# Attention over 512 heads on one core: chunks of 8 heads loaded in runs of three, and matmuls that use weights already in the array

## Chip, cores and metric

The kernel runs on one core of a Trainium2 chip. The metric is the device time of one execution in microseconds (us). The core has a matmul engine (PE, with its weight loads listed apart as PEld), a vector engine (DVE), a scalar engine (ACT), GpSimd (POOL), and SyncE (SP), which here only issues DMAs. The DMAs run on 16 engines that all queues share.

## The reference

For each of 16 x 32 = 512 heads, 192 queries attend to 1024 keys, with 128 elements a head, in bf16:

```python
B, H, Sq, Sk, D = 16, 32, 192, 1024, 128
scale = q.shape[-1] ** -0.5
scores = jnp.einsum("bhqd,bhkd->bhqk", q, k) * scale
p = _softmax(scores, axis=-1)
return jnp.einsum("bhqk,bhkd->bhqd", p, v)
```

## The kernel before

**Units.** Two heads a and b have 2 x 192 = 384 query rows. They are worked on as three units of 128 rows: unit `k3 = 0` has the first 128 rows of a, unit 1 the last 128 rows of b, and unit 2 the 64 rows left over from each, side by side in the two halves of the array (`tile_position` (0,0) and (0,64)). Three units make a pair of heads; there are 256 pairs and `NU` = 768 units.

**What happens to a unit.** PE multiplies queries by keys into `s_ps` (`qk`, lines 246, 253, 259: two matmuls of 512 columns, or four of half the array). DVE scales them into `ss` and takes the row extreme `nb` (line 335). Then half of the units (`route` R_W, never `k3 = 2`) go through POOL, which subtracts (line 210), and the others through ACT, which takes the exponential and the row sum (line 391), both into `x_sb`. PE transposes `x_sb` in eight blocks into `pt_ps` (`tr`, line 275). ACT moves that to `pt_sb` (line 402 with the exponential for R_W units, line 404 as a copy). PE multiplies with v into `o_ps` (`pv`, eight products, line 302, or twice eight in the array's halves, lines 308 and 310). For R_W units each of the eight is followed by a product of the same weights with one column of ones, which sums the rows (line 305). DVE divides each finished pair by its sums into `ob` (`onorm`, lines 362 and 365).

**Order on PE.** It is written out by hand: step `t` issues `qk(t+1)`, `tr(t-4)`, `pv(t-7)` (`LAGS`). `s_ps`, `pt_ps` and `o_ps` have two buffers each, `ss` four, `x_sb` four and `pt_sb` four. Each engine waits on counting semaphores (`s_qk`, `s_max`, `s_xp`, `s_xa`, `s_tr`, `s_eva`, `s_pv`, `s_on`) for its inputs and for free buffers. Every `pe.matmul` and `pe.transpose` becomes a weight load and a matmul; a wait that stands in front is on the load.

**Loads and stores.** Heads are taken in groups of `G` = 16 (32 groups of 24 units) and `kt`, `qt`, `vs` and `ob` have two slots each (`NS`, `NSO`). SP issues everything, in program order: k and q by a transposing DMA (`load_kq`, lines 144 and 148), v by a plain copy (`load_v`, line 155), the results from `ob` (`stores`, line 173). The k and q load of group g+2 waits until `qk` of group g is finished, its v load until `pv` of group g is finished. Group 0 is loaded in three parts (`FIRST`: heads 0 to 2, 2 to 8, 8 to 16). In the steady state SP's order is k, q and v of group g+2, then the store of group g:

```python
for g in range(NGR):
    if g + NS < NGR:
        loads(g + NS)
    for a, b in (LAST if g == NGR - 1 else ((0, PPG),)):
        stores(g, a, b)
```

Of the kernel before, what the change touches and what calls it, by code (L numbers as in the profile page):

```python
# [10 lines left out]
R_EA = 0  # L11
# [1 line left out]
R_W = 2  # L13


def _attention_kernel(nc, q, k, v, out, G=16, NS=2, LAGS=(2, 4, 5, 7), ROUTES=(R_W, R_W, R_EA, R_W, R_EA, R_EA),
                      FIRST=((0, 2), (2, 8), (8, 16)), LAST=((0, 4), (4, 6), (6, 7), (7, 8))):
    B, H, SQ, D = q.shape
    SK = k.shape[2]
    assert D == 128 and SK == 1024 and SQ == 192, (D, SK, SQ)  # L20
# [11 lines left out]
    NSS = L_X + 2  # L32
    NX = L_TR - L_X + 2
    NPT = L_PV - L_EV + 2
    NSO = 2
    NRS = 4

    qf = q.rearrange("b h s d -> (b h) s d")
# [25 lines left out]
    with ExitStack() as es:  # L64
# [74 lines left out]
        @block.sync  # L139
        def _(e):  # L140
            def load_kq(g, a, b, sems):
                s = g % NS
                h0 = g * G
                e.dma_start_transpose(  # L144
                    kt[:, s, :, a * 128:b * 128],
                    kf[h0 + a:h0 + b].rearrange("g (p t) d -> (g p) (t d)", t=KT_TILES),
                ).then_inc(sems[0], 16)
                e.dma_start_transpose(  # L148
                    qt[:, s, a * SQ:b * SQ],
                    qf[h0 + a:h0 + b].rearrange("g r d -> (g r) d"),  # L150
                ).then_inc(sems[1], 16)

            def load_v(g, a, b, sm):
                h0 = g * G
                e.dma_start(  # L155
                    vs[:, g % NS, a:b],
                    vf[h0 + a:h0 + b].rearrange("g (p t) d -> p g t d", t=KT_TILES),
                ).then_inc(sm, 16)

            def loads(g):  # L160
                s = g % NS
                last_u = (g - NS + 1) * UPG - 1
                if g >= NS:
                    e.wait_ge(s_qk, last_u + 1)
                load_kq(g, 0, G, (sxk[s], sxq[s]))
                if g >= NS:
                    e.wait_ge(s_pv, last_u + 1)
                load_v(g, 0, G, svl[s])

            def stores(g, a, b):  # L170
                so = g % NSO
                e.wait_ge(s_on, g * PPG + b)
                e.dma_start(
                    of[g * G + 2 * a:g * G + 2 * b].rearrange("h r d -> (h r) d").rearrange(
                        "(n p) d -> p n d", p=128),
                    ob[:, so, a:b].rearrange("p pg y d -> p (pg y) d"),
                ).then_inc(sst[so], 16)

            n = len(FIRST)
            for i in range(n):  # L180
                load_kq(0, *FIRST[i], (sf[i], sf[i]))
                if i > 0:
                    for i2 in range(i if i > 1 else 0, i + 1):
                        load_v(0, *FIRST[i2], sfv[i2])
            for g in range(1, min(NS, NGR)):
                loads(g)
            for g in range(NGR):
                if g + NS < NGR:
                    loads(g + NS)
                for a, b in (LAST if g == NGR - 1 else ((0, PPG),)):  # L190
                    stores(g, a, b)
            for so in range(min(NSO, NGR)):
                n_uses = len(range(so, NGR, NSO))
                if so == (NGR - 1) % NSO:
                    n_uses += len(LAST) - 1
                e.wait_ge(sst[so], 16 * n_uses)
# [21 lines left out]

        @block.tensor
        def _(pe):  # L220
            def qk(u):
                pr, k3, g, pg = unit_info(u)
                s = g % NS
                a = 2 * pg
                b = 2 * pg + 1
                if g == 0:
                    for i, (h, _) in enumerate(FIRST):
                        if u == 3 * h // 2:
                            pe.wait_ge(sf[i], 32)
                elif u % UPG == 0:  # L230
                    pe.wait_ge(sxk[s], load_cnt(g))
                    pe.wait_ge(sxq[s], load_cnt(g))
                if u >= 2:
                    pe.wait_ge(s_max, u - 1)
                S = s_ps[u % 2]
                ins = None
                for c in range(2):
                    cs = slice(4 * c, 4 * c + 4)

                    def keys(x):  # L240
                        return kt[:, s, cs, x * 128:x * 128 + 128]

                    if k3 < 2:
                        x = a if k3 == 0 else b
                        x0 = a * SQ if k3 == 0 else b * SQ + 64
                        ins = pe.matmul(  # L246
                            S[:, cs],
                            qt[:, s, x0:x0 + 128],
                            keys(x),
                            start=True, stop=True,  # L250
                        )
                    else:
                        pe.matmul(  # L253
                            S[0:64, cs],
                            qt[:, s, a * SQ + 128:a * SQ + 192],
                            keys(a),
                            start=True, stop=True, tile_position=(0, 0),
                        )
                        ins = pe.matmul(  # L259
                            S[64:128, cs],  # L260
                            qt[:, s, b * SQ:b * SQ + 64],
                            keys(b),
                            start=True, stop=True, tile_position=(0, 64),
                        )
                ins.then_inc(s_qk, 1)

            def tr(u):
                wait_x(pe, u)
                if u >= 2:
                    wait_evac(pe, u - 2)  # L270
                X = x_sb[:, u % NX, :]
                PT = pt_ps[u % 2]
                ins = None
                for t in range(KT_TILES):
                    ins = pe.transpose(PT[:, t, :], X[:, t * 128:t * 128 + 128], ident[:])  # L275
                ins.then_inc(s_tr, 1)

            def pv(u):
                pr, k3, g, pg = unit_info(u)
                s = g % NS  # L280
                if g == 0:
                    for i, (h, _) in enumerate(FIRST):
                        if u == 3 * h // 2:
                            pe.wait_ge(sfv[i], 16)
                elif u % UPG == 0:
                    pe.wait_ge(svl[s], load_cnt(g))
                wait_evac(pe, u)
                if k3 == 0 and pr >= 2:
                    pe.wait_ge(s_on, pr - 1)
                O = o_ps[pr % 2]  # L290
                PTS = pt_sb[:, u % NPT]
                sl = O_SLOT[k3]
# [1 line left out]
                b = 2 * pg + 1  # L294
                ins = None
                with_rs = route(u) == R_W
                for t in range(KT_TILES):
                    first = t == 0
                    last = t == KT_TILES - 1
                    if k3 < 2:  # L300
                        x = a if k3 == 0 else b
                        ins = pe.matmul(O[:, sl, :], PTS[:, t, :], vs[:, s, x, t, :],  # L302
                                        start=first, stop=last, skip_group_check=True)
                        if with_rs:
                            ins = pe.matmul(O[:, 3, sl: sl + 1], PTS[:, t, :], ones[:, 0:1],  # L305
                                            start=False, stop=last, skip_group_check=True)
                    else:
                        pe.matmul(O[0:64, sl, :], PTS[:, t, 0:64], vs[:, s, a, t, :],  # L308
                                  start=first, stop=last, skip_group_check=True, tile_position=(0, 0))
                        ins = pe.matmul(O[64:128, sl, :], PTS[:, t, 64:128], vs[:, s, b, t, :],  # L310
                                        start=first, stop=last, skip_group_check=True, tile_position=(0, 64))
                        if with_rs:
                            pe.matmul(O[0:64, 3, sl: sl + 1], PTS[:, t, 0:64], ones[:, 0:1],
                                      start=False, stop=last, skip_group_check=True, tile_position=(0, 0))
                            ins = pe.matmul(O[64:128, 3, sl: sl + 1], PTS[:, t, 64:128], ones[:, 0:1],
                                            start=False, stop=last, skip_group_check=True, tile_position=(0, 64))
                ins.then_inc(s_pv, 1)

            pe.wait_ge(s_setup, 2)
# [1 line left out]
            for step in range(NU + L_PV):  # L321
                if step + 1 < NU:
                    qk(step + 1)
                if 0 <= step - L_TR < NU:
                    tr(step - L_TR)
                if 0 <= step - L_PV < NU:
                    pv(step - L_PV)

        @block.vector
        def _(dve):  # L330
# [120 lines left out]
```

## Time and profile before

| | |
|---|---|
| median of 3 runs | 1224.64 us (1224.64 to 1226.19) |
| the profiled execution | 1224.55 us, its span 1222.8 us |
| PE busy | 1168.8 us, 96% of the span |
| DVE, ACT, POOL busy | 1096.5, 1002.2, 722.7 us |
| weight loads (PEld) busy | 905.4 us, x19456 |
| bytes moved by DMA | 321.76 MB, mean 263 GB/s |
| DMA issues of k, q, v, results | 34, 34, 34, 35 |

The span runs from the first to the last instruction that the profiler recorded; the rest of an execution's time lies around it. A PE row's duration includes the pipeline, so PE's pace is read from the starts of matmuls or from their number in a stretch, not from durations. In a view of stretches ("windows"), a row holds the stretch in us, its length, the busy time and number of instructions of PE, PEld, DVE, ACT and POOL, the granted share of PE's clock, the share of the DMA engines' time and GB/s. In the timeline of SP's queue, a row holds start, duration, line and DMA; the duration is that of the issue, which lasts while the queue has no room. "q1" is the queue of the program's DMAs, "q8 instruction" one that brings instructions.

### The profile page before, as it was taken

The page shows a single profiled execution, that of the slowest core. Times are in us where ns is not written, and L with a number is a line of the kernel's source. Part 1 is how long each engine was busy: PE and PEld are TensorE (multiplying, and loading weights), DVE is VectorE, ACT ScalarE, POOL GpSimd, SP SyncE. Part 2 cuts the span into 40 slices and gives each one's busy share as a digit, 9 for nine tenths or more (in the row PEclk, how much of TensorE's full clock was granted, in tenths as well). Part 3 has the DMA queues.
Part 4 walks back from the last instruction along what each step waited for, and adds up shares of the span by engine and source line. Part 5 has one row for each costly group of instructions (what it writes and reads, how often), then busy time and mean ns, then how long its engine had stood idle before and what let it go on. Part 6 is the DMA issues. An engine that isn't in the chain of part 4 may idle for free.

```text
span 1222.8 us, 46686 instructions
## 1 busy us (share of the span) xinstructions
PE 1168.8 (96%) x19456; PEld 905.4 (74%) x19456; DVE 1096.5 (90%) x2304; ACT 1002.2 (82%) x1537; POOL 722.7 (59%) x390
## 2 busy tenths in 40 slices
PE   4699999999999999999999999999999999999998
PEld 2477777777777777777777777777777777777777
DVE  4589999999899998999999999889989999899896
ACT  3578888888888887888888888888878888888887
POOL 3356656666556655665665566556656666565664
PEclk9899999999999999999999999999999999999999
DMA  9999999999999999999999999999999999999991
GB/s 232 238 267 287 286 279 263 256 283 270 273 283 240 265 291 261 280 285 235 278 285 270 283 253 247 285 277 271 287 238 266 283 284 274 250 247 291 278 274 32
DMA packets 789920, 321.76 MB, mean 263 GB/s; under 512 B 724176, under 2 KB 724176, under 8 KB 789712
## 3 DMA queue, kind: packets, MB, share of 16 engines
q1 hardware_dynamic: 789712, 318.78, 111.9%
q8 instruction: 156, 2.56, 0.8%
q14 instruction: 52, 0.43, 0.1%
HBM read 134.22 MB, written 25.17 MB: 130 GB/s over the span
## 4 chain that ended last, share of the span: by engine, by line
PE 82%; DMA 11%; SPq 4%; issue 2%; ACT 0%; DVE 0%; ACTq 0%
PE pt_ps L275 26%; PE o_ps L302 21%; PE s_ps L246 17%; PE o_ps L308 10%; DMA vs<-in_v_dram 9%; PE s_ps L253 8%; DMA kt<-in_k_dram 2%; SPq L148 2%; SPq L144 2%; PE o_ps L305 1%; PE o_ps L310 0%; SPq L155 0%; PE s_ps L259 0%; ACT x_sb L391 0%; ACT pt_sb L402 0%
## 5 line engine op out<-in xcount | busy, mean ns | idle before, releaser
L335 DVE TENSOR_SCALAR_CACHE_REDUCE ss<-s_ps 128x1024 f32<-128x1024 f32 x768 | 933.4, 1221 | 108.9 <-PE s_ps L246 96.5
L210 POOL TENSOR_TENSOR x_sb<-ss,nb 128x1024 bf16<-128x1024 f32 x384 | 722.0, 1894 | 487.8 <-PE pt_ps L275 474.8
L275 PEld LDWEIGHTS pt_ps<-ident,x_sb 128*128 128x128 bf16 x6144 | 387.3, 98 | 230.2 <-issue 111.4
L402 ACT ACTIVATE pt_sb<-pt_ps 128x1024 bf16<-128x1024 bf16 x384 | 390.9, 1018 | 102.3 <-PE pt_ps L275 102.3
L275 PE MATMUL pt_ps<-ident,x_sb 128*128 128x128 bf16 x6144 | 472.9, 220 | 1.1 <-ACT pt_sb L402 0.8
L391 ACT ACTIVATE x_sb<-ss,nb 128x1024 bf16<-128x1024 f32 x384 | 438.4, 1142 | 9.0 <-DVE ss L335 9.0
L302 PE MATMUL o_ps<-vs,pt_sb 128*128 128x128 bf16 x4096 | 382.2, 218 | 3.2 <-DMA vs<-in_v_dram 3.2
L246 PE MATMUL s_ps<-kt,qt 128*128 128x512 bf16 x1024 | 308.0, 382 | 45.5 <-issue 29.9
L302 PEld LDWEIGHTS o_ps<-vs,pt_sb 128*128 128x128 bf16 x4096 | 325.5, 97 | 4.9 <-DMA vs<-in_v_dram 4.6
L404 ACT ACTIVATE pt_sb<-pt_ps 128x512 f32<-128x512 f32 x384 | 228.6, 595 | 103.7 <-PE pt_ps L275 103.6
L305 PE MATMUL o_ps<-ones,pt_sb 128*128 128x1 bf16 x3072 | 282.0, 165 | 0.0
L305 PEld LDWEIGHTS o_ps<-ones,pt_sb 128*128 128x128 bf16 x3072 | 255.5, 96 | 0.0
L308 PE MATMUL o_ps<-vs,pt_sb 128*64 128x128 bf16 x2048 | 162.4, 222 | 0.0
L310 PE MATMUL o_ps<-vs,pt_sb 128*64 128x128 bf16 x2048 | 162.4, 222 | 0.0
L253 PE MATMUL s_ps<-kt,qt 128*64 128x512 bf16 x512 | 153.2, 381 | 1.0 <-DVE ss L335 0.9
L259 PE MATMUL s_ps<-kt,qt 128*64 128x512 bf16 x512 | 153.2, 381 | 0.0
L365 DVE TENSOR_TENSOR ob<-o_ps,rinv 128x384 bf16<-128x384 f32 x256 | 142.7, 557 | 8.7
L308 PEld LDWEIGHTS o_ps<-vs,pt_sb 128*64 128x64 bf16 x2048 | 121.0, 109 | 26.6 <-issue 0.2
L310 PEld LDWEIGHTS o_ps<-vs,pt_sb 128*64 128x64 bf16 x2048 | 121.0, 109 | 0.0
L246 PEld LDWEIGHTS s_ps<-kt,qt 128*128 128x128 bf16 x1024 | 67.6, 97 | 49.5 <-issue 39.3
L391 ACT ACTIVATION_READ_ACCUMULATOR x_sb<-ss,nb 128x1 f32 x384 | 74.2, 193 | 0.0
L335 DVE DVE_READ_ACCUMULATOR ss<-s_ps 128x1 f32 x768 | 63.7, 83 | 0.0
(11 smaller groups left out, 166.2 us busy)
## 6 DMA issues: line engine op xcount, KB each, us to landing
vs<-in_v_dram SPq DMA_DIRECT2D x31, 4096.0 KB, 15.2
out_dram<-ob SPq DMA_DIRECT2D x31, 768.0 KB, 17.3
vs<-in_v_dram SPq DMA_DIRECT2D x1, 2048.0 KB, 9.7
vs<-in_v_dram SPq DMA_DIRECT2D x1, 1536.0 KB, 8.4
kt<-in_k_dram SPq DMA_TRANSPOSE x34, 31.0
qt<-in_q_dram SPq DMA_TRANSPOSE x34, 6.2
vs<-in_v_dram SPq DMA_DIRECT2D x1, 512.0 KB, 5.0
out_dram<-ob SPq DMA_DIRECT2D x1, 384.0 KB, 3.2
```

Of the source, the lines that this page charges most:

```text
L210: gp.tensor_tensor(x_sb[:, u % NX, :], ss[:, u % NSS, :], nb[:, u % NSS: u % NSS + 1].to_broadcast([128, SK]), ALU.subtract,).then_inc(s_x ...
L246: ins = pe.matmul(S[:, cs], qt[:, s, x0:x0 + 128], keys(x), start=True, stop=True,)
L253: pe.matmul(S[0:64, cs], qt[:, s, a * SQ + 128:a * SQ + 192], keys(a), start=True, stop=True, tile_position=(0, 0),)
L275: ins = pe.transpose(PT[:, t, :], X[:, t * 128:t * 128 + 128], ident[:])
L302: ins = pe.matmul(O[:, sl, :], PTS[:, t, :], vs[:, s, x, t, :], start=first, stop=last, skip_group_check=True)
L305: ins = pe.matmul(O[:, 3, sl: sl + 1], PTS[:, t, :], ones[:, 0:1], start=False, stop=last, skip_group_check=True)
L308: pe.matmul(O[0:64, sl, :], PTS[:, t, 0:64], vs[:, s, a, t, :], start=first, stop=last, skip_group_check=True, tile_position=(0, 0))
L310: ins = pe.matmul(O[64:128, sl, :], PTS[:, t, 64:128], vs[:, s, b, t, :], start=first, stop=last, skip_group_check=True, tile_position=(0, ...
L335: dve.tensor_scalar(ss[:, u % NSS, :], s_ps[u % 2][:].rearrange("p t k -> p (t k)"), -scale, None, ALU.mult, ALU.min, accum_out=nb[:, u % ...
L391: act.activation(x_sb[:, u % NX, :], ss[:, u % NSS, :], ACT_FN.Exp, bias=nb[:, u % NSS: u % NSS + 1], scale=-1.0, accum_out=rs[:, pr % NRS ...
L402: act.activation(pt_sb[:, u % NPT], pt_ps[u % 2][:], ACT_FN.Exp, scale=-1.0).then_inc(s_eva, 1)
L404: act.activation(words(pt_sb[:, u % NPT]), words(pt_ps[u % 2][:]), ACT_FN.Copy).then_inc(s_eva, 1)
```

## The change

Loads come in chunks of `G` = 8 heads (64 chunks of 12 units), with four slots in each ring (`NS` and `NSO` = 4; the same number of heads as before for k, q and v). After chunk 0 (in two parts), chunk 1, and chunks 2 and 3, SP takes three chunks at a time (`RUN`): k and q of all three, then stores of finished chunks up to three before the run, then v of all three, then stores up to the chunk before the run. In the code, a run that begins with chunk 1 is followed by the store of chunk 0.

On PE, loads of weights and products are issued apart. `qk` loads a query block once for its two products, and the row-sum product uses the weights of the v product ahead of it. The waits are spread: a load waits for its own operand, and the first product behind it for the space it writes to or for the other operand. In a step, `pv` stands ahead of `tr`, and it works on unit t-8 (`LAGS` ends in 8), so `pt_sb` has five buffers.

```diff
-def _attention_kernel(nc, q, k, v, out, G=16, NS=2, LAGS=(2, 4, 5, 7), ROUTES=...,
-                      FIRST=((0, 2), (2, 8), (8, 16)), LAST=((0, 4), (4, 6), (6, 7), (7, 8))):
+def _attention_kernel(nc, q, k, v, out, G=8, NS=4, RUN=3, LAGS=(2, 4, 5, 8), ROUTES=...,
+                      FIRST=((0, 2), (2, 8)), LAST=((0, 2), (2, 3), (3, 4))):
...
-    NSO = 2
+    NSO = 4
...
-            def loads(g):
+            def next_kq(g):
                 s = g % NS
-                last_u = (g - NS + 1) * UPG - 1
                 if g >= NS:
-                    e.wait_ge(s_qk, last_u + 1)
+                    e.wait_ge(s_qk, (g - NS + 1) * UPG)
                 load_kq(g, 0, G, (sxk[s], sxq[s]))
+
+            def next_v(g):
                 if g >= NS:
-                    e.wait_ge(s_pv, last_u + 1)
-                load_v(g, 0, G, svl[s])
+                    e.wait_ge(s_pv, (g - NS + 1) * UPG)
+                load_v(g, 0, G, svl[g % NS])
...
+            runs = [[1], [2, 3]]
+            rest = list(range(4, NGR))
+            runs += [rest[i:i + RUN] for i in range(0, len(rest), RUN)]
+            stored = 0
+            for run in runs:
+                for g in run:
+                    next_kq(g)
+                while stored < run[0] - 2:
+                    stores(stored, 0, PPG)
+                    stored += 1
+                for g in run:
+                    next_v(g)
+                while stored < run[0]:
+                    stores(stored, 0, PPG)
+                    stored += 1
+            for g in range(stored, NGR):
                 for a, b in (LAST if g == NGR - 1 else ((0, PPG),)):
                     stores(g, a, b)
...
+            def product(o, w, x, at=(0, 0), start=True, stop=True, transpose=False):
+                return pe.add_instruction(mybir.InstMatmult(
...
+                    ldweights=False,
+                ))
...
                 for c in range(2):
                     cs = slice(4 * c, 4 * c + 4)
...
+                    for at, ps_, x, w in tiles:
+                        if c == 0:
+                            pe.ldweights(w, tile_position=at)
+                            if at[1] == 0:
+                                if g > 0 and u % UPG == 0:
+                                    pe.wait_ge(sxk[s], load_cnt(g))
+                                if u >= 2:
+                                    pe.wait_ge(s_max, u - 1)
+                        ins = product(S[ps_, cs], w, kt[:, s, cs, x * 128:x * 128 + 128], at)
                 ins.then_inc(s_qk, 1)
...
+                    w = X[:, t * 128:t * 128 + 128]
+                    pe.ldweights(w, is_transpose=True, tile_position=(0, 0))
+                    if t == 0 and u >= 2:
+                        wait_evac(pe, u - 2)
+                    ins = product(PT[:, t, :], w, ident[:], transpose=True)
...
+                        w = PTS[:, t, rows]
+                        pe.ldweights(w, tile_position=at)
...
+                        ins = product(O[rows, sl, :], w, vs[:, s, x, t, :], at, first, last)
                         if with_rs:
+                            ins = product(O[rows, 3, sl: sl + 1], w, ones[:, 0:1], at, False, last)
...
                     qk(step + 1)
+                if 0 <= step - L_PV < NU:
+                    pv(step - L_PV)
                 if 0 <= step - L_TR < NU:
                     tr(step - L_TR)
-                if 0 <= step - L_PV < NU:
-                    pv(step - L_PV)
```

## The prediction

> **What bounds the kernel now.** I read the page first, then the windows view in stages of 100 us, then the timeline of SP's queue, then the windows view in stretches of a few microseconds with the DMA view beside it, and last the timeline of TensorE (PE).
>
> ```profile
> PE 1168.8 (96%) x19456; PEld 905.4 (74%) x19456; DVE 1096.5 (90%) x2304; ACT 1002.2 (82%) x1537; POOL 722.7 (59%) x390
> DMA  9999999999999999999999999999999999999991
> q1 hardware_dynamic: 789712, 318.78, 111.9%
> q8 instruction: 156, 2.56, 0.8%
> ```
> Two things are full at once: PE at 96%, and the DMA engines at 9 in every slice but the last. The page's chain names PE; which of the two sets the pace must be read by stage.
>
> ```profile
> 100.00:200.00 100.00, 100.00 (x1686) 77.96 (x1684) 95.00 (x200) 86.64 (x133) 62.05 (x33) 1.00 1.16 275
> 200.00:300.00 100.00, 99.64 (x1681) 77.68 (x1678) 94.47 (x200) 86.28 (x134) 62.05 (x33) 1.00 1.13 274
> 300.00:400.00 100.00, 96.00 (x1620) 74.52 (x1620) 90.49 (x190) 82.67 (x128) 60.42 (x33) 1.00 1.15 266
> ```
> The second column is PE with its matmuls. A unit has 19456/768 = 25.33 of them, so from 100 to 300 us, without a gap, PE needs 200/(3367/25.33) = 1.505 us a unit, 36.1 us for a group of 24. From 300 on it has gaps.
>
> ```profile
> 99.01 26.92 SPq L144 DMA_TRANSPOSE kt<-in_k_dram  x1
> ...
> 581.55 26.83 SPq L144 DMA_TRANSPOSE kt<-in_k_dram  x1
> 608.43 4.10 SPq L148 DMA_TRANSPOSE qt<-in_q_dram  x1
> 612.57 0.58 SPq L155 DMA_DIRECT2D vs<-in_v_dram  x1
> 613.20 4.44 SPq L173 DMA_DIRECT2D out_dram<-ob  x1
> 617.70 28.35 SPq L144 DMA_TRANSPOSE kt<-in_k_dram  x1
> ...
> 1141.01 26.85 SPq L144 DMA_TRANSPOSE kt<-in_k_dram  x1
> ```
> SP's queue is never empty: each issue starts as the last ends. (The view of waits books 806 us of SP's L144 as waiting for PE, but group 1's k load at 29.5 us, which has no wait in the program, took 25.35 us too; it is the transfer that holds the issue.) From group 3 to group 31 it takes (1141.01 - 99.01)/28 = 37.2 us a group, over PE's 36.1. So after the start the DMA sets the pace, and PE loses about 1.1 us a group.
>
> **What a group's 37.2 us are made of.**
>
> ```profile
> 594.50:603.00 8.50, 8.50 (x145) 6.52 (x143) 8.05 (x19) 7.30 (x13) 5.13 (x4) 1.00 1.25 283
> 603.00:605.50 2.50, 2.50 (x53) 2.04 (x49) 2.21 (x3) 1.74 (x4) 1.64 (x2) 1.00 1.33 147
> 615.50:625.00 9.50, 9.50 (x167) 7.52 (x166) 9.05 (x19) 8.29 (x15) 6.06 (x4) 1.00 1.05 393
> 501.00:504.00 3.00, 3.00 (x55) 2.42 (x54) 2.71 (x5) 2.24 (x5) 2.14 (x3) 1.00 1.28 289
> 56.25:58.25 2.00, 0.00 (x0) 0.00 (x0) 0.00 (x0) 0.00 (x0) 0.00 (x0) 0.50 1.13 160
> ```
> The last column is GB/s. Transposed loads run at 290, v copies at 393, never mixed. 16 heads of k and q are 4.98 MB (17.2 us), their stores 0.79 MB (2.7 at 290), their v 4.19 MB (10.7): 30.6 us. In 603 to 605.5 the DMA view shows one 16 KB packet of the instruction queue, and the rate halves: 2.5 x (1 - 147/290) = 1.2 us lost; the stretch 565.5 to 567.5, with another, has 115 GB/s, 1.2 too. So each fetch of instructions stops the transposes 1.2 to 1.3 us. In 615.5 to 625, with v moving, there is one as well and the rate stays at 393. The page has 156 fetches, 4.9 a group; v moves for some 13 of the 37 us, so two thirds meet transposes or stores: 3.3 x 1.3 = 4.3 us. 37.2 - 30.6 - 4.3 = 2.3 us are left for switching between transposes and copies and for the step from kt to qt.
>
> **The change, part by part**, per 24 heads (36 units, one run), which now take 1.5 x 37.2 = 55.8 us of DMA; the bytes stay.
>
> Fewer instructions. 1,024 weight loads in qk and 3,072 in front of the ones product go, and most of PE's 1,058 separate semaphore instructions, since the waits are spread over loads and products; the program order of the changed kernel leaves about 34,950 of 39,970. Fetches fall from 156 to 137, 0.92 fewer per run, x 2/3 x 1.3 = -0.8 us.
>
> Fewer switches. One k-to-v and v-to-k pair per 24 heads in place of 1.5. The pair costs between nothing and the 2.3 left over; I take 1.8, near the upper end, because the crossing from kt to qt shown above loses nothing: -0.9 us (0 to -1.15).
>
> More steps between transposes. Three of kt to qt in place of 1.5, and two of qt to the next kt where there were none: 3.5 more. The last two rows bound one: 501 to 504 crosses from kt to qt at 289 GB/s and loses nothing; 56.25 to 58.25 crosses at 160 and loses 0.9. The nearest rows are the steady ones, where a fetch close by mostly covers the step and SP has queued ahead: I take 0.15, +0.5 us, and keep 0 and 0.9 (0 to +3.2 us) for the range. The 124 added DMAs bring issues, not bytes; SP's queue has them under the transfers.
> By the Trainium skill (DMA: Bandwidth & Descriptors, Anatomy of one DMA) a DMA carries about 2.0 us of fixed cost at any size. Unhidden, that is an estimate of 248 us for 124 more; the crossing at 289 GB/s says that it is hidden here.
>
> Sum: 55.8 - 0.8 - 0.9 + 0.5 = 54.6 us a run, against PE's 36 x 1.505 = 54.2. Over 21.3 runs: -1.2 x 21.3 = -26 us.
>
> PE itself. Removed loads lie beside matmuls:
>
> ```profile
> 520.79 0.22 PE L302 MATMUL o_ps<-vs,pt_sb 128*128 128x128 bf16 x1
> ...
> 520.85 0.17 PE L305 MATMUL o_ps<-ones,pt_sb 128*128 128x1 bf16 x1
> ...
> 520.88 0.22 PE L302 MATMUL o_ps<-vs,pt_sb 128*128 128x128 bf16 x1
> ```
> v product to ones product 60 ns, ones to the next about 30. Without its load the second could shrink to nothing (3,072 x 30 ns = 92 us off PE at most) or not at all; while the DMA sets the pace neither shows. I count zero. The change of order keeps half-array pv beside half-array qk, so entries to that mode stay as many.
> By the Trainium skill (TensorE: Matmul & The Clock Gate, the section on 56 and 53.3 ns) no two matmuls start closer than about 25 ns; by that the gain is under 5 ns each, 15 us of PE.
>
> The start loses. SP now issues the store of chunk 0 ahead of chunk 2's k load. That store waits until 12 units are normalised; pv of unit 11 stands behind qk of unit 20, whose keys land near 31 us (the issue of heads 8 to 16 ends at 28.84), so about 31 + 8 x 1.5 + 2 = 45, while the DMA would be free at about 37: +8 us, with everything of SP's behind it. Later stores wait for the chunk before the run, and PE ends that while two more v loads (11 us) run: covered by about 8 us.
>
> The end loses. The last group's v lands some 36 us before the end now. In the last run the first v lands 11 us before the third and PE then has 36 units, 54 us: 54 - 11 - 2 = 41, +5 us. pv one step later adds half a unit, within this.
>
> Span: 1222.8 - 26 + 8 + 5 = 1209.8. The profiled execution took 1224.55, 1.75 over its span, and the median of the runs is 1224.64; so 1211.5, said as 1211.
>
> **The rivals.**
> *Steps between transposes are not covered (slower).* A step costs 0.31 us where gain and losses balance (-1.7 + 3.5 x 0.31 = -0.6 a run, -13 in all). At 0.6, two thirds of the bad row: 55.8 - 1.7 + 2.1 = 56.2, +9 + 13 = 1246; at 0.9 it is 1269. For it: small transposes at the start (5 to 7.5 us: 150 GB/s) also lose. Against: the steady crossing.
> *The DMA falls below PE.* If the steps are free and a fetch is met less often, the run is 54.2 or less and PE's rate holds: -1.6 x 21.3 = -34, + 5 for the end; the start's 8 us are made good, since the DMA then has time over: span 1194, 1195.
> *Nothing that shows.* The DMA's gain (-13) is eaten by the start and end: 1222 to 1227.
>
> **How the numbers follow.** Forecast 0.47, low steps or PE's rate 0.11, nothing 0.09, uncovered steps 0.33. The range 1192 to 1246 takes in the first three and the rival up to steps of 0.6. About 0.2% (2.4 us) is what a measurement can tell from no change. Faster 0.58, same 0.09, slower 0.33.
>
> **What would show it.** Right: some 137 packets of the instruction queue; three kt/qt pairs in a row on SP with no dip under 250 GB/s at the steps that have no fetch; runs 54 to 55 us apart; PE waiting for the first v of a run; a gap of some 8 us in the DMA near 40 us. Wrong: dips at each qt to kt, runs of 56 us or more, or fetches that stop copies too; or weight loads that no longer hide, with transposes on PE more than 56 ns apart.

## The result, and the profile after

The changed kernel took 1256.30 us (median of four, 1252.29 to 1259.79); the kernel before took 1224.64 us beside it. The ratio is 1.0267, with a 95% interval of 1.0217 to 1.0318: 33 us slower, where 1211 us, 14 us faster, had been forecast. The profiled execution took 1259.79 us, with a span of 1257.8.

The page, in the same lines as before (engines; DMA digits and GB/s in 40 slices; two DMA queues; the chain by engine):

```profile
PE 1182.4 (94%) x19456; PEld 886.3 (70%) x15360; DVE 1077.3 (86%) x2304; ACT 1004.0 (80%) x1537; POOL 722.2 (57%) x390
...
DMA  9699999999999999999999999999999999999971
GB/s 237 161 268 254 284 263 252 310 224 295 220 305 257 261 290 242 308 224 283 227 299 228 289 269 260 301 227 292 223 304 217 301 266 257 301 229 295 220 250 34
...
q1 hardware_dynamic: 792688, 318.79, 109.8%
q8 instruction: 136, 2.23, 0.7%
...
PE 76%; DMA 19%; SPq 4%; issue 0%; ACT 0%; DVE 0%; ACTq 0%; DVEq 0%
```

PE still has its 19,456 matmuls, with 4,096 fewer weight loads, and the instruction queue brought 136 packets where 156 had been. The DMA is full except in the second slice and at the end. The chain now has 19% of DMA in it, 11% before. The windows say the same by stage (second column: PE and its matmuls; last three: clock, DMA share, GB/s):

```profile
100.00:200.00 100.00, 87.81 (x1433) 65.79 (x1131) 79.59 (x170) 73.58 (x113) 52.63 (x28) 0.93 1.18 274
200.00:300.00 100.00, 95.34 (x1592) 71.98 (x1258) 88.47 (x191) 82.60 (x128) 60.13 (x32) 0.98 1.18 266
700.00:800.00 100.00, 99.70 (x1681) 75.11 (x1326) 92.05 (x199) 86.18 (x133) 62.08 (x34) 1.00 1.16 256
```

When nothing holds PE (700 to 800 us) it does 1681 matmuls in 100 us, as many as before. Elsewhere it waits for data. The view of waits names two:

```profile
PE o_ps L233 <- DMA vs<-in_v_dram: 43.9, 17, 11.2
PE s_ps L233 <- DMA qt<-in_q_dram: 26.1, 4, 11.9
```

One run of three chunks in the timeline of SP's queue (start, length, line, operation):

```profile
193.58 10.94 SPq L144 DMA_TRANSPOSE kt<-in_k_dram  x1
204.56 1.34 SPq L148 DMA_TRANSPOSE qt<-in_q_dram  x1
...
226.90 1.34 SPq L148 DMA_TRANSPOSE qt<-in_q_dram  x1
228.28 0.58 SPq L174 DMA_DIRECT2D out_dram<-ob  x1
228.91 7.62 SPq L155 DMA_DIRECT2D vs<-in_v_dram  x3
236.57 11.77 SPq L174 DMA_DIRECT2D out_dram<-ob  x2
248.39 10.62 SPq L144 DMA_TRANSPOSE kt<-in_k_dram  x1
```

The first k loads of the runs start at 80.31, 135.74, 193.58, and so on to 1157.28 us: (1157.28 - 80.31)/19 = 56.7 us a run, where 54.6 had been forecast and 55.8 is what 24 heads cost before.

To see which transfers carry that, I took for each DMA the time at which it landed (the median of its 16 completions) and counted it from the landing of the one before, between 150 and 1120 us, per 24 heads in us:

```
kernel             k      q     stores   v      sum
before            29.8   4.6    3.9    17.5    55.9
after             29.5   5.6    4.2    17.5    56.7
e1_pe_only        29.2   4.3    3.9    17.4    54.9
e4_first_store    29.1   5.4    4.2    17.4    56.1
e11_store2        29.3   4.2    4.0    17.4    54.9
e9_run2_store1    29.9   5.2    3.9    17.4    56.4
e10_run3_store1   29.4   4.9    4.0    17.2    55.4
e14_store_late3   28.3   5.3    5.6    17.0    56.3
```

Each row is one execution. `after` and `e4_first_store` (below) run the same program in this stretch and differ by 0.6, so a difference of that size between two rows says little by itself; the times of whole runs have to bear it out.

### The profile page after: what moved, and what is told of

Read it like the earlier page. It is cut to its first block, busy times and chain, and to the rows that moved or that the text cites. A ratio compares the mean times of both kernels' runs of the same rounds, so it can differ in the third digit from the quotient of the medians.

```text
span 1257.8 us, 41815 instructions
## 1 busy us (share of the span) xinstructions
PE 1182.4 (94%) x19456; PEld 886.3 (70%) x15360; DVE 1077.3 (86%) x2304; ACT 1004.0 (80%) x1537; POOL 722.2 (57%) x390
## 4 chain that ended last, share of the span: by engine, by line
PE 76%; DMA 19%; SPq 4%; issue 0%; ACT 0%; DVE 0%; ACTq 0%; DVEq 0%
PE o_ps L233 28%; PE pt_ps L233 25%; PE s_ps L233 23%; DMA vs<-in_v_dram 19%; SPq L144 3%; SPq L148 1%; DMA qt<-in_q_dram 0%; ACT x_sb L401 0%; DVE ss L345 0%; DVE ob L375 0%; SPq L155 0%; ACT pt_sb L412 0%; ACT pt_sb L414 0%; DVE rinv L372 0%; SPq L174 0%
## 5 line engine op out<-in xcount | busy, mean ns | idle before, releaser
L345 DVE TENSOR_SCALAR_CACHE_REDUCE ss<-s_ps 128x1024 f32<-128x1024 f32 x768 | 915.1, 1219 | 163.2 <-PE s_ps L233 93.7
L314 PEld LDWEIGHTS <-pt_sb 128*128 128x128 bf16 (+1 forms) x8192 | 479.9, 104 | 283.1 <-issue 208.8
L233 PE MATMUL o_ps<-vs,pt_sb 128*128 128x128 bf16 (+1 forms) x8192 | 544.1, 219 | 44.2 <-DMA vs<-in_v_dram 43.9
L233 PE MATMUL s_ps<-kt,qt 128*128 128x512 bf16 (+1 forms) x2048 | 474.3, 392 | 27.1 <-DMA qt<-in_q_dram 26.1
L288 PEld LDWEIGHTS <-x_sb 128*128 128x128 bf16 x6144 | 359.5, 98 | 26.8 <-issue 2.9
L233 PE MATMUL o_ps<-ones,pt_sb 128*128 128x1 bf16 x3072 | 287.6, 166 | 0.0
L272 PEld LDWEIGHTS <-qt 128*128 128x128 bf16 (+1 forms) x1024 | 79.2, 103 | 58.2 <-DMA qt<-in_q_dram 21.2
L372 DVE RECIPROCAL rinv<-o_ps 128x2 f32<-128x2 f32 (+1 forms) x256 | 42.1, 165 | 6.2 <-PE o_ps L233 6.2
L372 DVE RECIPROCAL rinv<-rs 128x1 f32<-128x1 f32 (+1 forms) x256 | 36.9, 144 | 0.0
```

The lines of the kernel that those rows point to most:

```text
L233: return pe.add_instruction(mybir.InstMatmult(name=nc.get_next_instruction_name(), engine=mybir.EngineType.PE, ins=[pe.lower_ap(x), pe.low ...
L272: pe.ldweights(w, tile_position=at)
L288: pe.ldweights(w, is_transpose=True, tile_position=(0, 0))
L314: pe.ldweights(w, tile_position=at)
L345: dve.tensor_scalar(ss[:, u % NSS, :], s_ps[u % 2][:].rearrange("p t k -> p (t k)"), -scale, None, ALU.mult, ALU.min, accum_out=nb[:, u % ...
L372: dve.reciprocal(rinv[:, pr % 2, sel], src[:, sel]).then_inc(s_ri, 1)
```

## The experiments

Theory S was that the new order of the DMAs costs the time and PE's new program costs nothing; rival P was that PE's program is slower itself. Times are given with the ratio to the kernel before on the same chip.

**Each half of the change alone.** `e1_pe_only` has PE's new program with the old loads and stores; `e2_loads_only` the reverse.

```
e1_pe_only:     G=16, NS=2, SP's program, FIRST and LAST of before; PE's program and LAGS of after
e2_loads_only:  G=8, NS=4, RUN=3, SP's program of after; PE's program of before, LAGS=(2, 4, 5, 7)
```

> The changed TensorE program (weights loaded once, pv ahead of the transposes, lag 8) with the loads and stores of the kernel before: groups of 16 heads, two slots. Theory S (the new schedule of the DMAs costs the time, TensorE's edits cost nothing): the DMA keeps its 37.2 us a group less what 20 fewer instruction packets give, so 1207 to 1225 us, first k loads of the groups 36.7 to 37.2 us apart, and about 137 packets of the instruction queue. Rival P (TensorE's new program itself is slower: in after the second pair of half-array qk products takes 236 ns where it took 212, and pv stands ahead of the transposes): 1240 us or more, with TensorE's gaps not put down to the DMA.

> The loads, stores, chunks and rings of the changed kernel with TensorE's program of the kernel before (a load for every product, transposes ahead of pv, lag 7). Theory S: the time of the changed kernel or up to 17 us more, 1253 to 1275 us, since the fetches go back to about 156 to 158, and the runs of three chunks stand 56.7 to 57.5 us apart. Rival P: 1220 to 1235 us.

`e1_pe_only` took 1206.23 us, ratio 0.9883 (0.9858 to 0.9909), with 136 packets and groups (1121.96 - 133.78)/27 = 36.6 us apart. `e2_loads_only` took 1257.93, ratio 1.0299 (1.0268 to 1.0330). So PE's half is a gain of 14 us and the loads' half loses as much as the whole change. Rival P is gone. `e1_pe_only` is also the best version in this study, level with `e11_store2` below. What did not fit: under the new loads PE's half gained nothing that can be measured (1.0299 against 1.0267).

**Is PE's gain the fetches?** `e8_reload` is `e1_pe_only` with a load ahead of every product again.

```
-                        if c == 0:
-                            pe.ldweights(w, tile_position=at)
+                        pe.ldweights(w, tile_position=at)
...
                         if with_rs:
+                            pe.ldweights(w, tile_position=at)
                             ins = product(O[rows, 3, sl: sl + 1], w, ones[:, 0:1], at, False, last)
```

> e1_pe_only with a weight load ahead of every product again (4,096 more instructions, the order of pv, transposes and lags of the changed kernel kept). Theory F (the 14 us that e1_pe_only gained are fetches of instructions that stop the transposing loads): about 152 packets of the instruction queue and 1216 to 1224 us. Rival O (the gain is the order of pv ahead of the transposes or the waits behind the weight loads): 1203 to 1210 us at 152 packets.

1226.74 us, ratio 1.0029 (1.0004 to 1.0055), with 152 packets; (1139.42 - 97.60)/28 = 37.2 us a group, as before. The same 100 us of full work on PE, in `e1_pe_only` and then in `e8_reload`:

```profile
100.00:200.00 100.00, 100.00 (x1689) 75.60 (x1333) 93.20 (x201) 86.75 (x134) 62.02 (x33) 1.00 1.18 267
```
```profile
100.00:200.00 100.00, 100.00 (x1686) 80.53 (x1684) 93.25 (x201) 86.58 (x133) 62.02 (x33) 1.00 1.15 264
```

351 more loads in the window (third column), and PE does its matmuls at the same rate. So the loads cost PE nothing, and the order of `pv` and `tr` gains nothing. What else differs is the instruction queue: by the ratios, 0.0146 x 1221 = 17.8 us for 16 packets, 1.1 us each.

**Stores.** Three kernels move stores of the changed kernel: `e3_no_mid_store` takes the store between q and v away from there, `e4_first_store` lets chunk 0's store go out later (behind the v of chunks 2 and 3, with chunk 1's), and `e5_run3` does both (chunk 0's store goes behind the v of chunks 2 and 3).

```
# e3 and e5
-                while stored < run[0] - 2:
-                    stores(stored, 0, PPG)
-                    stored += 1
# e4
-                while stored < run[0]:
+                while stored < run[0] and run[0] > 1:
# e5
-                while stored < run[0]:
+                while stored < run[-1] - 2:
```

> The changed kernel, but the one store that each run issues between its q and its v loads goes behind the v loads, with the two others. Theory S, with the crossings as they read in after's packets (q to store 0.75 us and store to v 1.51 where q to v took 0.87 before): 1.4 us less for each of 20 runs, so 28 us less, 1225 to 1235 us, runs 55.3 us apart. Rival T (the loss is the 3.5 extra steps between transposes, and the store's crossing only moves to another place): 1248 to 1258 us, runs 56.4 us apart or more.

> The changed kernel, but the store of chunk 0 does not stand ahead of the k load of chunk 2; it goes out with the first run of three. Theory S: the 11.5 us in which the DMA stood still from 36.6 us on are gone, and the time falls by 8 to 12 us to 1244 to 1248, the later runs still 56.7 us apart. Rival: TensorE or the slots of the ring hold chunk 2's load or a later one by as much, the gap turns up a run later, and the time stays at 1254 to 1258.

> The changed kernel with both stores moved: none between the q and the v loads of a run, and the store of chunk 0 behind the v loads of chunks 2 and 3. The two alone gave 11 and 18 us. Theory S (each takes its own crossing of the DMA): the gains add, 1225 to 1232 us, runs of 24 heads 55.7 to 56.0 us apart, so still slower than the kernel before by the steps between transposes. Rival (both took the same waiting, since a mid-run store only costs where TensorE is late from the start): 1236 to 1242 us.

`e3_no_mid_store` took 1244.92 us, ratio 1.0192 (1.0164 to 1.0220), a gain of 9 us by the ratios where 28 had been expected. `e4_first_store` took 1238.17, 1.0145 (1.0120 to 1.0170), a gain of 15, more than expected. `e5_run3` took 1243.24, 1.0176 (1.0123 to 1.0229): the two gains do not add, and with the start mended no gain of moving the mid-run store can be measured (1.0145 where it was, 1.0176 moved). So the 1.4 us a run that I had read off the rates around its crossing are not gained by moving it. That does not make the store free: in `e3_no_mid_store` and `e5_run3` it goes out as the third in a row behind v, and the runs with one store below price all three.

The start shows plainly. SP's queue in the changed kernel:

```profile
27.34 1.29 SPq L155 DMA_DIRECT2D vs<-in_v_dram  x1
47.14 0.39 SPq L174 DMA_DIRECT2D out_dram<-ob  x1
47.57 9.37 SPq L144 DMA_TRANSPOSE kt<-in_k_dram  x1
```

and the windows from 38 to 47 us, in the changed kernel and in `e4_first_store` (last column GB/s):

```profile
38.00:47.00 9.00, 9.00 (x156) 6.80 (x121) 8.20 (x18) 7.63 (x13) 5.63 (x4) 1.00 0.01 3
```
```profile
38.00:47.00 9.00, 9.00 (x153) 6.81 (x120) 8.03 (x19) 7.13 (x11) 5.38 (x3) 1.00 1.27 221
```

SP waits with a store from 28.63 to 47.14 us, and from 36.6 us on the DMA stands still. No packet of the program's queue (q1) starts between 36.6 and 48.1 us: 11.5 us lost.

**Length of a run.** `e6_run2` and `e7_run1` are `e5_run3` with `RUN=2` and `RUN=1`.

> As e5_run3, but runs of two chunks: 16 heads, as the kernel before loads them, in twice as many DMAs. Theory S with crossings as the packets show them (a change k/q to v, store and back 2.1 us, a step from q to the next k 0.35): half a change more and half a step less per 24 heads, +0.9 us, so 1243 to 1252 us; against e1_pe_only, which has the same order with one DMA for both chunks, the difference is the price of the extra steps (kt to qt and qt to kt, 1.5 of each per 24 heads). Rival (a change of kind costs no more than a step): the time of e5_run3 within 4 us. Rival L (long runs hold v back and TensorE waits for it): faster than e5_run3 by 8 us or more.

> As e5_run3, but runs of one chunk: k, q, v, store for 8 heads at a time. Theory S: two changes more and two steps less per 24 heads than runs of three, +3.5 us, so 1295 to 1310 us. Rival (a change costs no more than a step): the time of e5_run3 within 6 us. The slope over runs of three, two and one gives the price of a change less a step: 0.5 and 2 more of them per 24 heads.

`e6_run2` took 1231.94 us, 1.0074 (1.0046 to 1.0102): faster than runs of three, as rival L had it, against my forecast. `e7_run1` took 1291.61, 1.0546 (1.0488 to 1.0605). A change between kinds of transfer is dear in the step from two chunks to one, and looks free in the step from three to two. So something in runs of three was eating its gain. In `e5_run3` a run issues three stores in a row, in `e6_run2` two, in `e7_run1` one.

**One store per run.** `e9_run2_store1` and `e10_run3_store1` are `e6_run2` and `e5_run3` with the chunks of a run stored by one DMA (for runs of three with a ring of six); `e14_store_late3` cuts that store into three again, behind the one wait; `e11_store2` cuts the store of `e1_pe_only` in two.

```
# e9, e10: bt is the list of chunks that one DMA stores
-                e.wait_ge(s_on, g * PPG + b)
+                e.wait_ge(s_on, bt[-1] * PPG + b)
...
-                    ob[:, so, a:b].rearrange("p pg y d -> p (pg y) d"),
+                    ob[:, so:so + n, a:b].rearrange("p s pg y d -> p (s pg y) d"),
# e14: after the same wait
+                for i in range(n):
+                    g = bt[i]
+                    e.dma_start(of[g * G + 2 * a:g * G + 2 * b]..., ob[:, so + i, a:b]...)
# e11
-                for a, b in (LAST if g == NGR - 1 else ((0, PPG),)):
+                for a, b in (LAST if g == NGR - 1 else ((0, PPG // 2), (PPG // 2, PPG))):
```

> e6_run2 with the two stores of a run as one DMA (slots of the ring of outputs side by side), so loads in twice as many DMAs as e1_pe_only and stores in as many. Theory B (a step between two stores costs as the packets show it, 0.82 us): 1.5 fewer per 24 heads, some 20 us, so 1208 to 1216 us, and only a few us are left over e1_pe_only for the steps between transposes. Rival K (the steps between transposes cost it all, 3 more per 24 heads at 0.4): 1228 to 1236 us, as e6_run2.

> e5_run3 with the three stores of a run as one DMA (a ring of six outputs in place of four). Theory B: two steps between stores fewer per 24 heads, at 0.8 us 30 us less, 1209 to 1217 us, runs 54.8 to 55.2 us apart. Rival K: 1238 to 1246 us.

> e10_run3_store1 with the store cut into three DMAs again, all three behind one wait for the last finished chunk of the run. Theory N (the number of stores costs, 22 us between e5_run3 and e10_run3_store1): 1238 to 1247 us. Rival T (what cost was that the pieces went out one by one, between the v copies and the next k, and not their number): 1217 to 1226 us.

> e1_pe_only with each group's store split into two DMAs of half the size, the suspected cost by itself, one more step between stores per 16 heads. Theory B: 32 steps at 0.8 us, so 26 us more, 1228 to 1236 us. Rival K (a step between stores costs nothing of its own): 1204 to 1211 us.

`e10_run3_store1` took 1221.02 us, 1.0010 (0.9987 to 1.0033), 20 us less than `e5_run3` by the ratios. `e14_store_late3` took 1238.48, 1.0140 (1.0101 to 1.0179): cutting the store gives 16 us back, so in runs of three it is the number of stores that costs (theory N), 16 us over 40 more DMAs, 0.4 us each. The changed kernel has its three stores in another place, one between q and v and two behind v. `e4_first_store`, which has them there too, takes as long as `e14_store_late3` (1.0145 and 1.0140), so that place is no cheaper.

But `e9_run2_store1` took 1226.65, 1.0050 (1.0023 to 1.0077), only 3 us under `e6_run2`, and `e11_store2` took 1206.36, 0.9889 (0.9848 to 0.9930), the time of `e1_pe_only`: in those orders a store cut in two costs little or nothing. So theory B's 0.8 us for every step between two stores is wrong, and the cost belongs to three stores in a run of three chunks. Whether the third store brings it or the three v copies ahead of the stores was not tried: no kernel with runs of three chunks stores them in two DMAs. The ring of six outputs, which came with the one store, does not show (`e5_run3` with four 1.0176, `e14_store_late3` with six 1.0140, intervals overlapping). SP's queue with one store (`e10_run3_store1`), with three (`e14_store_late3`), and with two behind the one v copy of 16 heads (`e11_store2`):

```profile
378.66 3.46 SPq L170 DMA_DIRECT2D vs<-in_v_dram  x3
388.64 3.48 SPq L190 DMA_DIRECT2D out_dram<-ob  x1
392.16 19.66 SPq L159 DMA_TRANSPOSE kt<-in_k_dram  x1
```
```profile
387.65 7.58 SPq L170 DMA_DIRECT2D vs<-in_v_dram  x3
400.03 10.55 SPq L192 DMA_DIRECT2D out_dram<-ob  x3
410.62 10.32 SPq L159 DMA_TRANSPOSE kt<-in_k_dram  x1
```
```profile
386.29 0.58 SPq L155 DMA_DIRECT2D vs<-in_v_dram  x1
386.91 12.87 SPq L173 DMA_DIRECT2D out_dram<-ob  x2
399.83 18.59 SPq L144 DMA_TRANSPOSE kt<-in_k_dram  x1
```

With one store, the next k is issued at 392.16 us, 11.0 us before the store lands (403.16). With three, SP is held for 10.55 us by the stores, and k is issued at 410.62, 2.8 us before the last store lands (413.39). The late issue of k would be an easy cause, but `e11_store2` speaks against it: its two stores hold SP for 12.87 us, its k is issued at 399.83, 2.7 us before the second store lands (402.55), and it loses nothing. In the table of landings the three stores of `e14_store_late3` take 1.6 us more per run than the one of `e10_run3_store1`, q 0.4 more, and k gets 1.1 back. Why three stores cost stays open.

**Starts of transposing DMAs.** `e15_k_halves` is `e1_pe_only` with each k load in two DMAs. `e12_kkkqqq` is `e10_run3_store1` with all k of a run ahead of all q.

```
# e15
+                w = (b - a) // parts
+                for c in range(a, b, w):
                     e.dma_start_transpose(
-                        kt[:, s, :, a * 128:b * 128],
+                        kt[:, s, :, c * 128:(c + w) * 128],
...
# e12
-                for g in run:
-                    next_kq(g)
+                for g in run:
+                    next_k(g)
+                for g in run:
+                    next_q(g)
```

> e1_pe_only with each k load cut into two transposing DMAs of 8 heads: one more start of a transposing DMA per 16 heads and nothing else. Theory D (such a start costs 0.42 us, the difference of e9_run2_store1 and e1_pe_only over three starts): 31 starts, 13 us more, 1216 to 1223 us. Rival (a start behind a transposing DMA of the same tensor is covered): 1203 to 1210 us, so that the cost lies in the change of tensor or of row length.

> e10_run3_store1 with the loads of a run in the order k, k, k, q, q, q, v, v, v in place of k, q, k, q, k, q, v, v, v; the number of DMAs stays. Theory D (every start of a transposing DMA costs some 0.4 us, whatever stood before): within 5 us of e10_run3_store1. Rival X (the crossing from kt to qt costs, 0.7 to 0.9 us in the packets, not the DMA): two such crossings fewer per run, 20 runs, 15 to 30 us less than e10_run3_store1.

`e15_k_halves` took 1213.60 us, 0.9937 (0.9911 to 0.9964): 0.0054 x 1220 = 6.6 us over `e1_pe_only` for 31 starts, 0.21 us each. That is between the two expectations, and 1213.60 lies under what theory D asked for. `e9_run2_store1` against `e1_pe_only` has two more starts for each of 31 groups: 0.0167 x 1220 = 20.4 us, 0.33 each, the split of v included. But its end is shorter: from the landing of the last v (the last of its 16 completions) to the end of the span it has 1225.3 - 1196.3 = 29.0 us, `e1_pe_only` 1203.5 - 1167.4 = 36.1. In the table of landings, which leaves the ends out, it needs 56.4 - 54.9 = 1.5 us more for three starts, 0.5 each, and k and q carry it. So a start costs 0.2 to 0.5 us; why those of `e9_run2_store1` are the dearer ones stays open. `e12_kkkqqq` took 1233.15, 1.0115 (1.0058 to 1.0172), 13 us more and not 15 to 30 less than `e10_run3_store1`: rival X is wrong, crossing from kt to qt is not dearer than from kt to kt. Its runs are (1122.22 - 173.75)/17 = 55.8 us apart, the other's (1114.70 - 171.43)/17 = 55.5. PE waits longer for q (54.1 us against 13.7), which now lands behind three k, and no longer for v (29.1 us in `e10_run3_store1`); its waits for data are 11 us longer in all.

**Where PE's gain went.** `e13_store1_old_pe` is `e10_run3_store1` with PE's program of the kernel before.

```
e13_store1_old_pe:  SP's and DVE's programs of e10_run3_store1; PE's program of before, LAGS=(2, 4, 5, 7)
```

> e10_run3_store1 with the TensorE program of the kernel before. Under the old loads the new program gave 14 us (e1_pe_only), under the loads of the changed kernel 2 us (e2_loads_only against after). Theory M (the gain of fewer fetches was hidden by the stores in pieces, and comes back with one store): 1232 to 1240 us. Rival R (in runs of three the fetches fall into the transposes whatever the stores do, so fewer of them give nothing): 1217 to 1225 us.

1236.63 us, 1.0139 (1.0089 to 1.0188), 16 us over `e10_run3_store1` with 156 packets in place of 136. So with one store per run the gain of fewer fetches is back, and rival R is wrong: theory M, as far as this goes. The start is mended in these two runs as well, so which of the two hid the gain in the changed kernel was not separated.

## Why the prediction was wrong, point by point

**What bounds the kernel: right.** The DMA sets the pace before and after, and PE's own rate did not move. Of the signs written down, the 137 packets (136), PE's waits for v and the gap near 40 us came; so did runs of 56 us or more, a sign of being wrong. Most of the 45 us between forecast and result lie there: (56.7 - 54.6) x 20 = 42 us.

**Fewer instructions: right by itself, not in the changed kernel.** 17 us were forecast (0.8 x 21.3). Taken alone they are 14 (`e1_pe_only`) or 16 (`e10_run3_store1` against `e13_store1_old_pe`), with 136 packets where 137 had been forecast. In the changed kernel itself this gain did not show (1.0267, and 1.0299 with the old program); the stores in pieces or the start hid it.
The Trainium skill (TensorE: Matmul & The Clock Gate, the section on 56 and 53.3 ns) has no two matmuls start closer than about 25 ns, so that a removed load would hardly be seen on PE. The traces agree: from the start of a v product to that of the ones product the median is 55 ns, and from there to the next v product 26 ns, in the kernel before and in `e1_pe_only` alike; the two windows above have 1689 matmuls without the loads and 1686 with them.

**Fewer switches: right in size.** 19 us were forecast, 1.8 a pair. `e10_run3_store1` has 10 fewer than `e9_run2_store1` and as many more starts from q to k, and its last v lands at 1177.1 us where the other's lands at 1196.3: 1.9 us for a pair over a start, 2.1 to 2.4 for the pair. `e7_run1` against `e9_run2_store1`, both with one store per run, gives 0.0496 x 1221/30 = 2.0 over a start.

**More steps between transposes: too small.** The term took 0.15 us a step from the one steady crossing that lost nothing; the runs showed 0.2 to 0.5. For the 3.5 x 20 = 70 steps that is 15 to 35 us, not 11. The slow rival named this mechanism, and its break-even of 0.31 lies within what was measured; its 0.6 lies above it.
The Trainium skill (DMA: Bandwidth & Descriptors, Anatomy of one DMA) gives about 2.0 us of fixed cost per DMA, fitted there to DMAs that GpSimd issues; here SP issues them. In a queue that is kept full, 0.2 to 0.5 us showed here for one more transposing DMA; taken in full it would have asked for 31 x 2.0 = 62 us in `e15_k_halves` (an estimate from the page), which lost 6.6.

**Stores: the step that failed.** The prediction put the kernel's 124 added DMAs at nothing ("issues, not bytes", under the transfers), and its sum for a run has no term for the stores. The 16 heads' one store became two of half the size, three per run. One store per run in place of three is worth 16 to 20 us (`e14_store_late3`, `e4_first_store` and `e5_run3` against `e10_run3_store1`), 0.8 to 1.0 us a run: with it and the mended start, `e10_run3_store1` is level with the kernel before. With 0.8 to 1.0 for the stores and 0.2 to 0.5 a step in place of 0.15, the forecast's 54.6 us a run become 55.6 to 56.8; 56.7 were measured.

**The start: right in kind, too small.** 8 us were forecast for the store ahead of chunk 2's k load; the DMA stood still for 11.5, and taking that store away gave 15.

**The end: right.** From the landing of the last v (the last of its 16 completions) to the end of the span it was 1222.8 - 1187.3 = 35.5 us before and is 1257.8 - 1216.5 = 41.3 after; 41 were forecast, and 5.8 more than before where 5 had been. A long run gives back at the end much of what it saves on the way: the last v of `e10_run3_store1` lands 19.2 us ahead of that of `e9_run2_store1`, and its end is 1219.1 - 1177.1 = 42.0 us, 13.0 longer.

Together, with the runs' prices: -14 for the fetches, +15 to 35 for the starts of transposing DMAs, -22 for the switches (2.2 x 10), +16 to 20 for the stores, +11 to 15 at the start, +6 at the end: +12 to +40 us, with 33 measured. The parts do not add exactly, as `e3_no_mid_store`, `e4_first_store` and `e5_run3` show, and the 14 us for the fetches did not show in the changed kernel itself, so the sum is a check of sizes and no more.

## What to carry to other kernels

Where one queue of DMAs sets the pace, count every DMA in it, the stores and those of a few hundred KB too, and give each kind a price of its own: the saved switch was real (2 us), and ten times 2 us went to small starts and to stores in three pieces. A gain that rests on fewer instructions can be taken without the reordering that came with it; here the PE half alone gives 0.9883 and the whole change 1.0267. And look at what a store in SP's order waits for before the first loads behind it: in the first 50 us nothing covers that wait.

## What the runs showed of the hardware

- A packet of the instruction queue cost 1.1 us of the kernel's time here, where the DMA sets the pace (17.8 us for 16 packets, `e8_reload` against `e1_pe_only`); apart from that, 4,096 weight loads showed no cost.
- One more transposing DMA in a full queue costs 0.2 us (`e15_k_halves`) to 0.5 us (`e9_run2_store1`); a change of tensor is no dearer than another DMA of the same (`e12_kkkqqq`).
- Two stores in a row cost as much as one of their size (1206.36 and 1206.23 us); three, behind three v copies, cost 16 us more than one over 20 runs. Why stays open: SP issues the next k 2.8 us before the last store lands there, but 2.7 us before it with the two stores that cost nothing.
- PE starts again at half its clock after a long wait: at the first run of three of `e4_first_store`, where it waits for v (14.4 us at the longest), the granted clock is 0.50. Behind that wait a v product and its ones product take 60 + 72 = 132 ns from start to start, where 55 + 26 = 81 are the medians.

```profile
110.00:120.00 10.00, 3.39 (x36) 2.56 (x22) 0.42 (x1) 0.60 (x1) 0.00 (x0) 0.50 1.03 359
```

The changed kernel has the same stretch from 120 to 130 us (0.50), in its longest wait for v (11.2 us). Its lower mean clock (0.974 against 0.991) goes with such waits; what the clock costs by itself was not tried.
